# Moving output stores, one product order and one PSUM bank in a two-stage attention and maxout kernel

## The chip, the cores and the metric

One core of a Trainium2 chip. The metric is device time in microseconds (us), the median of several runs. A profiled execution gives the times of single instructions.

## The reference

Two layers follow each other. The first is a gated linear recurrence over 768 steps, for 4 batches of 8 heads with 48 features; the second is a feed-forward layer with a maximum over three products.

```python
f = 1.0 / (1.0 + np.exp(-f_logit))
for t in range(S):
    state = f[:, :, t, :, None] * state + np.einsum('bhd,bhe->bhde', k[:, :, t], v[:, :, t])
    y[:, :, t] = np.einsum('bhd,bhde->bhe', q[:, :, t], state)
x = y.transpose(0, 2, 1, 3).reshape(B * S, H * D)          # 3072 x 384
h = np.maximum(np.maximum(x @ w1, x @ w2), x @ w3)          # 3072 x 768
out = h @ w_out                                             # 3072 x 384
```

## The kernel before

**Units and groups.** The recurrence is worked off in 24 units (`u`). A unit holds 64 steps of two batches, so 128 tokens. Four units make a group (`g`, 0 to 5) of 512 tokens, and a group goes through the feed-forward layer as a whole. In the main loop one unit of the recurrence is computed while the feed-forward work of the group before it is fed in between.

**How the order is set.** The order on every engine is the order in which the Python program emits the instructions; nothing is rearranged later. The feed-forward work of a group is a generator (`ffn_first` for group 0, `ffn` for the others) that yields after each piece of TensorE work with that piece's cost. `fill(ns)` draws pieces from the first pending generator until the given time is spent. So the statement after a `yield` is emitted when the next piece is drawn. Engines run their own queue in order and wait for each other by semaphores. All loads and stores but a few are issued by SP, whose queue is in order as well.

**A unit.** `load` and `load_v` fetch f, k, q and v; from unit 6 on f, k and q come for two units at a time, in eight DMAs for each of the three. `sigmoids` (ACT), `scan` (DVE, L329), `after` (kt by a DVE transpose L296, then kh on POOL L340), `before` (prod by a DVE scan L347, qt by L296, qh on POOL L351), `keys_by_blocks` (ks, DVE L382, in four parts), `pairs` (PE L396, masked to `at` by DVE L399), `values` (PE L415, then a one-element ACT copy `seen`, L422), `sums` (PE L433) and `finish` (PE L504, then ACT copies into xT, L511). `pack` moves a part of xT between partitions by DMA (L524). "k(10)" below is the load of k for units 10 and 11, "pairs(10)" the pairs of unit 10.

**Group 0.** `ffn_first` computes products of xT with w2 and w3 (`product`, L542), and it turns each 128-column piece of w1 by three TensorE transposes and an ACT copy (`turn`, L779 and L780). `linear` folds w1 into w_out (L787). `outputs` computes the four output tiles of the group (L568), ACT copies each into the buffer `o_four` (the tile `o`, L572), and `store` issues two DMAs for each (L560). In the text, product (5,1) is the one of the last block with w2, (5,2) the one with w3.

**Groups 1 to 5.** `inputs_by_pairs` computes the maxout in three blocks (n = 0, 1, 2) of seven products each (L883), which saves multiplications by sums and differences of the operands: `start`, `plain`, `fifth`, `sixth`, `seventh`, `third`, `fourth`. ACT copies partial results (L891, L897, L906, L911, L918), POOL adds (L901, L919), DVE forms the maxima (L926, L933, L934), POOL then makes the sums that the output needs (`sums_of_hm`, L608). `outputs_by_pairs` computes the output in the same manner (L636) in PSUM banks a, b and c. ACT reads bank a into `partial` (L641), DVE or POOL add the parts into `o_four` (L644, L703). Only when they are computed are the four tiles of a group put on the list `late`, and `store_late` issues their eight DMAs in the next group.

**Banks.** A product's bank comes from the pool `ps_f` (name p, two banks) or `ps_tr` (name tr, two banks), each in rotation. A bank is written again only when its last reader is done:

```python
def bank(in_tr=False):
    if in_tr:
        return ps_tr.tile([128, TOK], FP32, name="tr")
    return ps_f.tile([128, TOK], FP32, name="p")
```

Of the kernel before, what the change touches and what calls it, by code (L numbers as in the profile page):

```python
# [9 lines left out]
FP32 = mybir.dt.float32  # L10
# [45 lines left out]
def kernel(  # L56
# [15 lines left out]
    NU = B // 2 * (S // C)  # L72
# [4 lines left out]
    NJ = DFF // 128  # L77
    GRP = 4
    TOK = GRP * UT
# [10 lines left out]
    def fast():  # L90
        ctx = ExitStack()
        with ctx:
# [4 lines left out]
            ps_f = ctx.enter_context(tc.tile_pool(name="ps_f", bufs=2, space=bass.MemoryType.PSUM))  # L97
# [417 lines left out]
            def by_halves(xT):  # L515

                return xT[:, 0:NK].rearrange("p k t -> p (k t)").rearrange("p (two k t) -> p two k t", two=2, k=NK)
# [14 lines left out]
# [4 lines that stand above are left out]
# [17 lines left out]
            def new_top(w):  # L553
                return work.tile([128, TOK], FP32, name="top")[:, 0:w]

            def store(u, o):
                c, bp = divmod(u, 2)
                for a in range(2):
                    t0 = (2 * bp + a) * S + c * C
                    nc.sync.dma_start(out=out[t0:t0 + C, :], in_=o[a * C:(a + 1) * C, :])  # L560

            def outputs(hm, xT, i):
                p = bank()
                t = slice(i % 2 * UT, (i % 2 + 1) * UT)
                terms = [(hm[:, j, i * UT:(i + 1) * UT], w_out[:, j, :]) for j in range(NJ)]
                terms += [(by_halves(xT)[:, i // 2, k, t], w_nat[:, k, :]) for k in range(NK)]
                for n, (lhsT, rhs) in enumerate(terms):
                    nc.tensor.matmul(p[:, 0:DM], lhsT=lhsT, rhs=rhs, start=(n == 0), stop=(n == NJ + NK - 1))  # L568
                    if n % NK == NK - 1:
                        if n == NJ + NK - 1:  # L570
                            o = o_four[:, i]
                            nc.scalar.copy(o, p[:, 0:DM])  # L572
                            store(i, o)
                        yield NK * DM * COLUMN


# [17 lines left out]
            def mix_x(n):  # L594

                of = lambda k, c: w_lin[:, k, c * HD:(c + 1) * HD]
                dst, x, y = ((x_mix[2], of(1, 1), of(0, 1)), (x_mix[0], of(0, 1), of(0, 0)),
                             (x_mix[1], of(1, 1), x_mix[0]), (x_mix[3], of(1, 0), x_mix[1]),
                             (w_mix[4][:, 2], of(2, 0), of(2, 1)))[n]
                nc.gpsimd.tensor_tensor(dst, x, y, op=ALU.subtract)  # L600
# [9 lines left out]
            def sums_of_hm(hm, jj):  # L610
                sums_of_pair(hm[:, 2 * jj], hm[:, 2 * jj + 1], *(t[:, jj] for t in s_mix))
# [7 lines left out]
            def outputs_by_pairs(g, hm, xT):  # L619
# [9 lines left out]
                lin, lin_mix = [[w_lin[:, 2, half(n)]] for n in range(2)], [w_mix[4][:, 2]]  # L629
                partial = [w_nat[:, n, :] for n in range(NK)]  # L630
                last = g == NU // GRP - 1
                begun = set()

                def into(b, p, lhs, rhs, part=slice(None)):
# [11 lines left out]
                def second():  # L646
                    for p in range(2):
                        into(a, p, s2, T(1))
                        if p:
                            read(a, 1)  # L650
                        yield COST
# [25 lines left out]
                    store_part(g, 0, 0)  # L677
                yield 2 * PART_COST
                d = b if last else c
                if last:  # L680
                    yield from second()
                into(c, 0, s1, T(0))
                yield COST
# [6 lines left out]
                else:  # L690
                    nc.scalar.copy(tops[:, 2], c[:, 0:DM])
                yield COST
                if not last:
                    yield from second()
                into(a, 0, A(0, 1), T(2))
                yield COST
# [49 lines left out]
            late = []  # L746

            def store_late():
                while late:
                    store(*late.pop(0))  # L750
# [22 lines left out]

            def turn(j):

                p = ps_f.tile([128, TOK], FP32, name="p")
                piece = w_in[0][:, :, j * 128:(j + 1) * 128]
                for a in range(NK):
                    nc.tensor.transpose(p[:, a * 128:(a + 1) * 128], piece[:, a, :], ident)  # L779
                nc.scalar.copy(piece, p[:, 0:DM].rearrange("q (a c) -> q a c", a=NK))  # L780
                yield DM * COLUMN
# [89 lines left out]
            def inputs_by_pairs(g, hm, xT):  # L871
                X = lambda k, h: halves(xT, k, h)
                t1, t2, t3, t4, t5 = sums_of_x(g)
                s1, s2, s4 = w_sum
                s3 = w_two[1][:, 0]
                COST = 2 * HALF * COLUMN
                out = lambda n, h: hm[:, 2 * n:2 * n + 2, h * HALF:(h + 1) * HALF]
                first, u3 = rests[:, 0:2, 0:HALF], tops[:, 2:4, 0:HALF]
                A, B, U5 = {}, {}, {}

                def into(b, n, w, x, begin=False):
                    for j in range(2):
                        nc.tensor.matmul(b[:, j * HALF:(j + 1) * HALF], lhsT=w[:, (2 * n + j) * 128:(2 * n + j + 1) * 128],  # L883
                                         rhs=x, start=begin and j == 0, stop=True, skip_group_check=True)

                def plain(n):
                    B[n] = bank(True)
                    into(B[n], n, w_two[0][:, 1], X(1, 0), True)
                    yield COST
                    into(B[n], n, w_two[0][:, 2], X(2, 0))  # L890
                    nc.scalar.copy(out(n, 0), two(B[n]))  # L891
                    yield COST

                def start(n):
                    A[n] = bank()
                    into(A[n], n, w_two[0][:, 0], X(0, 0), True)
                    nc.scalar.copy(first, two(A[n]))  # L897
                    yield COST

                def join(n):  # L900
                    nc.gpsimd.tensor_tensor(out(n, 0), out(n, 0), first, op=ALU.add)  # L901

                def fifth(n):
                    into(B[n], n, s1, t1, True)
                    U5[n] = two(new_top(TOK))
                    nc.scalar.copy(U5[n], two(B[n]))  # L906
                    yield COST

                def sixth(n):
                    into(A[n], n, s2, t2)  # L910
                    nc.scalar.copy(out(n, 1), two(A[n]))  # L911
                    yield COST

                def seventh(n):
                    into(A[n], n, s3, t3)
                    yield COST
                    into(A[n], n, w_two[1][:, 2], X(2, 1))
                    nc.scalar.copy(u3, two(A[n]))  # L918
                    nc.gpsimd.tensor_tensor(u3, u3, U5[n], op=ALU.add)  # L919
                    yield COST  # L920

                def third(n):
                    into(B[n], n, s4, X(1, 1))
                    yield COST
                    into(B[n], n, w_two[0][:, 2], X(2, 1))
                    nc.vector.tensor_tensor(out(n, 1), two(B[n]), out(n, 1), op=ALU.add)  # L926
                    yield COST

                def fourth(n):
                    into(A[n], n, w_two[1][:, 1], t4)  # L930
                    yield COST
                    into(A[n], n, w_two[1][:, 2], t5)
                    nc.vector.scalar_tensor_tensor(out(n, 0), out(n, 0), 0.0, two(A[n]), op0=ALU.max, op1=ALU.max)  # L933
                    nc.vector.scalar_tensor_tensor(out(n, 1), out(n, 1), 0.0, u3, op0=ALU.max, op1=ALU.max)  # L934
                    sums_of_hm(hm, n)
                    if g == 1:
                        for i in ((0, 1), (2, 3, 4), ())[n]:
                            mix_x(i)
                    yield COST

                yield from start(0)
                yield from plain(0)
                join(0)
                store_late()
                yield from plain(1)
                yield from sixth(0)
                yield from fifth(0)
                for n in range(1, NJ // 2):
                    if n > 1:
                        yield from plain(n)  # L950
                    yield from seventh(n - 1)
                    yield from start(n)
                    join(n)
                    yield from third(n - 1)
                    yield from fifth(n)
                    yield from sixth(n)
                    yield from fourth(n - 1)
                yield from seventh(NJ // 2 - 1)
                yield from third(NJ // 2 - 1)
                yield from fourth(NJ // 2 - 1)  # L960
# [452 lines left out]
```

## Time and profile before

| what | value |
|---|---|
| median of three runs | 413.81 us (413.4 to 414.51) |
| the profiled execution | 413.13 us, span 411.4 us |
| granted TensorE clock | 0.998 |
| PE busy (matmuls) | 392.9 us, 96% of the span |
| DVE busy | 294.6 us, 72% |
| POOL busy | 245.7 us, 60% |
| ACT busy | 180.8 us, 44% |
| moved by DMA | 47.21 MB, mean 115 GB/s |

The span is the time from the first to the last instruction; the execution takes 1.73 us more. PE is the TensorE matmul, PEld its weight load, DVE is VectorE, ACT ScalarE, POOL GpSimd, and SPq the queue of SyncE, which here only issues DMAs. L560 is line 560 of the kernel. A PE row's end is modelled, and the rows of neighbouring matmuls overlap.

### The profile page before, as it was taken

To read this page: it belongs to the slowest core of one execution; us is meant where nothing else is said; L and a number is where in the kernel's file an instruction comes from. 1 tells how busy PE (TensorE), PEld (TensorE's weight loads), DVE (VectorE), ACT (ScalarE), POOL (GpSimd) and SP (SyncE) were. 2 spreads that over 40 slices of the span, in tenths; PEclk is the share of its full clock that TensorE was granted. 3 is DMA by queue.
4 is the path that set the end of the run, shared out by engine and by line. 5 is a ranking of instruction groups with operands and counts; after the bars stand their busy time and mean duration, and the time that the engine had idled before them with its cause. 6 is when DMAs were issued, how large, how long until landed. Compare 5 with 4: busy or idle time off the path is not lost.

```text
span 411.4 us, 11515 instructions
## 1 busy us (share of the span) xinstructions
PE 392.9 (96%) x4598; PEld 331.9 (81%) x4598; DVE 294.6 (72%) x569; ACT 180.8 (44%) x430; POOL 245.7 (60%) x270
## 2 busy tenths in 40 slices
PE   5988999999999989999999999999999999999995
PEld 4766765556678778998889998899988899988994
DVE  6997897996885899898898997998995450002500
ACT  2478786412224422425542345522354424586210
POOL 2189694843878777577495296667377850435700
PEclk9999999999999999999999999999999999999999
DMA  8999986776456775266655277734473003542012
GB/s 172 240 269 261 271 222 92 149 149 94 87 112 89 124 119 108 60 91 108 108 137 110 47 115 88 158 74 86 64 152 101 2 17 102 126 135 67 0 21 62
DMA packets 181562, 47.21 MB, mean 115 GB/s; under 512 B 160448, under 2 KB 179200, under 8 KB 181504
## 3 DMA queue, kind: packets, MB, share of 16 engines
q1 hardware_dynamic: 178032, 45.62, 54.1%
q10 hardware_dynamic: 3472, 0.81, 0.9%
q8 instruction: 37, 0.61, 0.6%
q14 instruction: 21, 0.17, 0.1%
HBM read 37.75 MB, written 4.72 MB: 103 GB/s over the span
## 4 chain that ended last, share of the span: by engine, by line
PE 85%; DVE 6%; POOL 3%; issue 2%; DMA 1%; ACT 1%; SPq 0%; DVEq 0%; POOLq 0%
PE p L883 17%; PE tr L883 15%; PE p L636 14%; PE tr L636 10%; PE p L542 7%; PE p L568 6%; PE p L787 3%; PE y L415 3%; PE a L396 3%; PE a L433 2%; PE y L504 2%; DVE ks L382 2%; PE tr L291 1%; POOL w_in L258 1%; DMA f_ld<-in_f_logit_dram 1%
## 5 line engine op out<-in xcount | busy, mean ns | idle before, releaser
L382 DVE STREAM_TRANSPOSE ks<-kh 32x128 f32<-32x128 f32 x256 | 77.3, 302 | 10.3 <-POOL kh L340 6.3
L883 PE MATMUL tr<-xT,placed 128*128 128x256 f32 x300 | 71.1, 382 | 0.0
L883 PEld LDWEIGHTS tr<-xT,placed 128*128 128x128 f32 x300 | 56.3, 190 | 8.0
L883 PE MATMUL p<-xT,placed 128*128 128x256 f32 x180 | 44.6, 379 | 0.0
L339 POOL COPY ends<-r 128x8 f32<-128x8 f32 x24 | 6.9, 288 | 56.9 <-DVE r L329 56.9
L340 POOL TENSOR_TENSOR kh<-kt,r 128x512 f32<-128x512 f32 x18 | 33.4, 1855 | 10.6 <-DVE kt L296 10.6
L883 PEld LDWEIGHTS p<-xT,placed 128*128 128x128 f32 x180 | 34.1, 190 | 4.7
L329 DVE TENSOR_TENSOR_SCAN r<-gate,from_one 128x520 f32<-128x520 f32 x24 | 33.4, 1391 | 5.9 <-ACT gate L308 2.8
L542 PE MATMUL p<-xT,w_in 128*128 128x256 f32 (+1 forms) x108 | 34.0, 459 | 3.4 <-POOL w_in L756 1.9
L511 ACT COPY xT<-y 64x256 f32<-64x256 f32 (+1 forms) x60 | 22.1, 369 | 23.3 <-PE y L504 22.6
L347 DVE TENSOR_TENSOR_SCAN prod<-gate,from_inv 128x520 f32<-128x520 f32 x24 | 30.5, 1269 | 0.0
L883 PE MATMUL p<-w_in,placed 128*128 128x256 f32 x120 | 30.4, 382 | 0.0
L644 DVE TENSOR_TENSOR o<-tr,w_in 128x384 f32<-128x384 f32 (+1 forms) x11 | 5.7, 521 | 34.3 <-PE tr L636 29.8
L608 POOL TENSOR_TENSOR w_in<-hm 128x256 f32<-128x256 f32 x15 | 11.1, 738 | 32.1 <-DVE hm L934 29.4
L542 PEld LDWEIGHTS p<-xT,w_in 128*128 128x128 f32 x108 | 19.5, 190 | 12.6 <-issue 6.0
L926 DVE TENSOR_TENSOR hm<-tr,hm 128x512 f32<-128x512 f32 x15 | 10.2, 683 | 23.1 <-ACT raw L280 17.2
L258 POOL TENSOR_TENSOR w_in<-top_bits,rest_bits 128x384 uint32<-128x384 uint32 x18 | 21.7, 1217 | 7.2 <-DVE top_bits L252 4.3
L883 PEld LDWEIGHTS p<-w_in,placed 128*128 128x128 f32 x120 | 22.4, 190 | 4.4 <-issue 1.3
L636 PE MATMUL p<-w_in,hm 128*128 128x192 f32 x120 | 25.3, 334 | 0.6 <-ACT w_in L641 0.6
L641 ACT COPY w_in<-p 128x384 f32<-128x384 f32 x15 | 7.2, 479 | 42.1 <-PE p L636 42.1
L280 ACT ACTIVATE raw<-top_bits 128x384 f32<-128x384 f32 x48 | 25.3, 526 | 0.4
L636 PE MATMUL tr<-w_out,w_in 128*128 128x192 f32 x120 | 24.4, 326 | 0.0
(156 smaller groups left out, 912.3 us busy)
## 6 DMA issues: line engine op xcount, KB each, us to landing
raw<-in_moe_w_dram SPq DMA_DIRECT2D x24, 384.0 KB, 4.2
v_ld<-in_v_dram SPq DMA_DIRECT2D x48, 96.0 KB, 3.3
placed<-in_moe_w_dram SPq DMA_DIRECT2D x12, 384.0 KB, 6.8
out_dram<-o SPq DMA_DIRECT2D x46, 96.0 KB, 2.2
placed<-in_moe_w_out_dram SPq DMA_DIRECT2D x6, 384.0 KB, 5.5
f_ld<-in_f_logit_dram SPq DMA_DIRECT2D x36, 64.0 KB, 2.7
k_ld<-in_k_dram SPq DMA_DIRECT2D x36, 64.0 KB, 2.6
q_ld<-in_q_dram SPq DMA_DIRECT2D x36, 64.0 KB, 2.6
```

What stands on the lines that cost most here:

```text
L258: nc.gpsimd.tensor_tensor(dst, by(top), by(rest), op=ALU.add)
L280: nc.scalar.activation(over, size, AF.Relu, scale=(-1 / HI_MIN, 1.0)[step - 1], bias=(1.0, -HI_END * (1 - 2.0 ** -24))[step - 1], accum_ou ...
L329: nc.vector.tensor_tensor_scan(r[:, 0:LEN][:, ::-1], flat(gate)[:, ::-1], flat(from_one)[:, ::-1], 1.0, op0=ALU.mult, op1=ALU.max)
L340: (nc.vector if u < BY_ROWS else nc.gpsimd).tensor_tensor(kh.rearrange("p h a t -> p a h t"), kt, by_batch(r[:, 1:LEN + 1].rearrange("p (x ...
L347: nc.vector.tensor_tensor_scan(flat(prod), flat(gate_tiles[u % 2]), flat(from_inv[u % 2]), 1.0, op0=ALU.mult, op1=ALU.max)
L382: nc.vector.transpose(ks[n * 32:(n + 1) * 32, :, par, e0:e0 + 32], kh[p0:p0 + 32, :, a, t0:t0 + 32])
L396: nc.tensor.matmul(p[t, par, hp * C:(hp + 1) * C], lhsT=kh[r, hp, a, :], rhs=qh[r, a, hp, :], start=True, stop=True)
L511: nc.scalar.copy(xT[o, :, t0 + a * C:t0 + (a + 1) * C], y[i, a, 0:HP * C].rearrange("p (h t) -> p h t", h=HP))
L542: nc.tensor.matmul(p if w < TOK else p.rearrange("p (two t) -> p two t", two=2), lhsT=w_in[i][:, kt, j * 128:(j + 1) * 128], rhs=x[:, t.st ...
L568: nc.tensor.matmul(p[:, 0:DM], lhsT=lhsT, rhs=rhs, start=(n == 0), stop=(n == NJ + NK - 1))
L636: nc.tensor.matmul(b[:, p * HD:(p + 1) * HD], lhsT=x, rhs=w, start=id(b) not in begun, stop=True, skip_group_check=True)
L883: nc.tensor.matmul(b[:, j * HALF:(j + 1) * HALF], lhsT=w[:, (2 * n + j) * 128:(2 * n + j + 1) * 128], rhs=x, start=begin and j == 0, stop= ...
```

## The change

There are three edits.

The four output tiles of group 0 are no longer stored by `outputs` when they are copied. They are put on `late`. In group 1 `store_late` is not called behind `join(0)`; it is called at the end of each turn of the loop over the blocks, so the eight DMAs are issued where the piece after the first block's last product (`fourth(0)`) is drawn. In groups 2 to 5 the call stays behind `join(0)`.

In `outputs_by_pairs` the two products with s2 (`second`) come ahead of the two with s1 in groups 4 and 5. Before, they did so in group 5 alone.

The last turn of a w1 piece (j = 5) takes its bank from the pool `ps_tr` instead of `ps_f`.

```diff
@@ outputs
                             nc.scalar.copy(o, p[:, 0:DM])
-                            store(i, o)
+                            late.append((i, o))
@@ outputs_by_pairs
                 last = g == NU // GRP - 1
+                tight = g >= NU // GRP - 2
...
                 d = b if last else c
-                if last:
+                if tight:
                     yield from second()
                 into(c, 0, s1, T(0))
...
-                if not last:
+                if not tight:
                     yield from second()
                 into(a, 0, A(0, 1), T(2))
@@ turn
-                p = ps_f.tile([128, TOK], FP32, name="p")
+                p = bank(j == NJ - 1)
@@ inputs_by_pairs
                 join(0)
-                store_late()
+                if g > 1:
+                    store_late()
                 yield from plain(1)
...
                     yield from sixth(n)
                     yield from fourth(n - 1)
+                    store_late()
                 yield from seventh(NJ // 2 - 1)
```

## The prediction

> **What bounds the kernel now.** First the page's busy row, then busy time by stage, with the stages cut where the maxout groups 1 to 4 begin on PE:
>
> ```profile
> PE 392.9 (96%) x4598; PEld 331.9 (81%) x4598; DVE 294.6 (72%) x569; ACT 180.8 (44%) x430; POOL 245.7 (60%) x270
> ...
> 118.47:180.89 62.42, 59.35 (x773) 53.32 (x773) 52.70 (x108) 23.86 (x57) 44.02 (x47) 1.00 0.59 100
> 180.89:239.38 58.49, 58.49 (x773) 53.20 (x773) 52.65 (x113) 24.42 (x60) 38.22 (x42) 1.00 0.57 99
> 297.89:356.19 58.30, 57.73 (x677) 51.85 (x677) 25.95 (x45) 26.01 (x67) 35.26 (x39) 1.00 0.32 79
> ```
>
> Columns: window, length, then busy us (and instructions) of PE, PEld, DVE, ACT, POOL, granted clock, DMA share, GB/s. PE is the bound, so a saving is worth the PE idle time that it removes. Group 1 runs the same 773 matmuls as group 2 and takes 62.42 - 58.49 = **3.93 us longer**, 3.07 of it visible as idle PE (62.42 - 59.35). Group 2 has no gap, group 4 has 0.57.
>
> Then PE's timeline, for the gaps (start, length, line; in brackets the idle time before and its releaser):
>
> ```profile
> 74.19 2.84 PE L542 MATMUL p<-xT,w_in 128*128 128x512 f32 x6 [0.35 <-ACT hm L807]
> ...
> 136.48 0.69 PE L396 MATMUL a<-qh,kh 48*64 48x64 f32 x32 [0.83 <-POOL qh L351]
> ...
> 153.87 0.66 PE L504 MATMUL y<-qh,state 48*48 48x64 f32 x32 [1.54 <-ACT seen L422]
> ...
> 161.71 1.19 PE L636 MATMUL p<-w_out,hm 128*128 128x192 f32 x4 [0.70 <-DVE hm L933]
> ...
> 345.98 0.92 PE L636 MATMUL p<-w_in,hm 128*128 128x192 f32 x4 [0.57 <-ACT w_in L641]
> ```
>
> Between 59.5 and 404 us PE has hardly another gap. For what is behind the first of group 1's, SP's timeline and DVE's:
>
> ```profile
> 113.74 1.33 SPq L164 DMA_DIRECT2D v_ld<-in_v_dram  x2
> 115.17 3.26 SPq L560 DMA_DIRECT2D out_dram<-o  x4
> 118.52 1.35 SPq L524 DMA_DIRECT2D xT<-xT  x2
> 119.96 1.40 SPq L164 DMA_DIRECT2D v_ld<-in_v_dram  x2
> 121.45 1.23 SPq L560 DMA_DIRECT2D out_dram<-o  x2
> 122.81 5.24 SPq L183 DMA_DIRECT2D k_ld<-in_k_dram  x8
> 128.14 4.15 SPq L183 DMA_DIRECT2D q_ld<-in_q_dram  x8
> 132.39 1.12 SPq L560 DMA_DIRECT2D out_dram<-o  x2
> ...
> 130.23 0.71 DVE L296 STREAM_TRANSPOSE kt<-k_ld 128x512 f32<-128x512 f32 x1 [2.55 <-DMA q_ld<-in_q_dram]
> 134.46 0.71 DVE L296 STREAM_TRANSPOSE qt<-q_ld 128x512 f32<-128x512 f32 x1 [2.39 <-DMA out_dram<-o]
> ```
>
> SP issues without a pause here, well behind the data: the pack at 118.52 copies an xT that ACT finished at 109.80. So k and q of units 10 and 11 are issued late. DVE idles 2.55 us for k and 2.39 for q (the profile names the last DMA event, a store, but qt reads q_ld, whose last issue ended at 132.29), POOL then makes qh, and pairs(10) waits for qh. The 4.9 us that DVE lost come back twice: DVE is nearly full from 135 to 162, and its late L934 holds ACT's copy L918 (5.94 us), behind which the small `seen` copy stands that releases L504; its late L933 gives the third gap. With the slow restart behind each, the excess of 3.93 divides so: the unit work from L415 to L504 takes 2.01 in group 2 (197.11 to 199.12 in the chain of waits), here 3.04 (134.51 to 137.55) and 3.76 (150.70 to 154.46), which is 1.03 and 1.75; 1.15 is left for the third.
>
> **What the Trainium skill says.** "Perfetto Trace Analysis", section "DMA Instruction — HWDGE (DVE, Sync)": a DMA's row starts when its semaphores are satisfied and ends when the sequencer is free for the next; moving the data lies outside. The trace agrees: q's rows take about 0.5 us, its data lands a median 2.5 us after issue. Section "What "DMA-bound" means" of that page lists an issuing sequencer that is solid with DMA rows as a bound of its own; SP from 108.8 to 148 is that, while the DMA share is 0.48 to 0.93. "PSUM — Partial Sum Buffer", section "Engine vs sequencer instructions": ACT, DVE and POOL queues are strict FIFO, and matmuls complete in program order. L918 ahead of `seen` is such a case.
>
> **The change, part by part.**
>
> *The last turn's bank.* Today product (5,1), the turn and product (5,2) take three of the two p banks in a row, so (5,2) at 74.19 waits for the copy L807 of (5,1), 73.55 to 74.14. With the turn in a tr bank, (5,2) takes the bank that L809 left at 71.73. The two tr banks were last read by DVE L351 (to 61.6) and ACT L369 (to 67.9), and are next asked for at 119, so the turn doesn't wait at 73.35. Linear(0) then needs the bank of (5,1), free at 74.14, and w1's last piece at its sixth matmul, about 78.1, copied by 75.96. Gain **0.35**; no new wait.
>
> *The stores.* Eight DMAs leave three places on SP. What follows starts earlier by 118.52 - 115.17 = 3.35, then 122.81 - 121.45 = 1.36, then 133.56 - 132.39 = 1.17, together 5.88. k(10) and q(10) are issued 4.71 earlier; their rooms were last read for unit 7 (DVE, before 104), so nothing else holds them. k's data is there at 130.23 - 4.71 = 125.5, q's at 134.46 - 4.71 = 129.75. DVE: its reciprocal ends at 127.68, kt to 128.4, prod 1.20 to 129.5, qt 129.75 to 130.4. POOL: the pack is 3.35 earlier, so L867's wait of 1.24 goes and all behind moves up by it: ends to 128.8, kh 2.02 to 130.8, qh 1.18 to 132.0. PE reaches pairs(10) at 135.65 - 0.35 = 135.3: 3.3 of slack, the 0.83 goes.
>
> What is late next is DVE's L933, which needs fourth(0) on PE, done at 134.2. L933 0.65, L934 1.3, a quarter of ks 1.26: at(10) starts at 137.4 instead of 141.53, 4.1 earlier. From at(10) to the release of L504 by `seen` the trace has 153.87 - 141.53 = 12.34: 149.8. PE is there at 152.33 - 0.83 - 0.35 = 151.15; the 1.54 goes with 1.4 of slack. The third: L933 of the last block ended at 161.65, now 157.5; PE comes at 161.01 - 2.72 = 158.3 by the visible gaps, at 157.9 with the slow restarts behind them. Slack 0.4 to 0.8, the thinnest; I leave a remainder of 0 to 0.5 here. So group 1 gains between 3.07 (gaps only) and 3.93 (as fast as group 2); I take **3.5**.
>
> The eight DMAs come back on SP where plain(2) of group 1 begins, behind v(12): v(12) ended at 152.4, now 146.5. Eight such stores in one burst take 5.07 at 303.84, so to 151.6. Behind them stand one check load (152.41 before), the pack of units 8 to 10, which waits for ACT until 155.38 before and about 152.3 after, and f(14) at 157.83. SP idled 2.35 ahead of that pack, so the burst fits where the gap and the 5.88 are. Who waits for the stores: DVE L644 of group 1, which overwrites `o`, due near 159; landing by 153.8 (2.2 after issue). Cost 0, covered by 5 us; at SP's old times the stores would land at 159.6 and cover nothing.
>
> *s2 first in group 4.* Today bank a carries s2 and then the next product back to back, so PE waits 0.57 for ACT's reading L641 (345.45 to 345.93). With s1's two products (2.6 us) between, that wait is hidden. The new place of s2 follows the reading of a at 338.81 to 339.29; between stand finish(23) (0.6) and b's rest (0.65), so s2 is due at 340.05: 0.7 of slack. Its POOL sums were ready at 335.97, its DVE ones at 336.3. In group 5, already in this order but without a finish between, the first s2 block is 0.25 longer, which bounds the cost; I take 0. L691's copy comes 2.6 later and is needed by bank c's next product, 3.3 after it. Gain **0.6** (0.57, and 0.11 for a slower restart). Group 5 doesn't change.
>
> **Sum:** 0.35 + 3.5 + 0.6 = 4.45; from 3.1 + 0.35 + 0.3 = 3.75 to 3.93 + 0.45 + 0.68 = 5.06. The profiled execution took 413.13 (span 411.4 and 1.73 around it); the sum makes it 408.7. The median is 0.68 above, so **409.4** there, full case 408.7 to 410.1.
>
> **Rivals.** *Half:* DVE, busy 26.8 of the 28 us from 136 to 164, doesn't catch up, and of the second and third gap half stays, or all: 1.03 for the first, 1.45 or 0 for the rest, 0.95 for the other two parts, 410.4 or 411.8. For it: the slack of 0.4. Against: group 2 does the same DVE work (52.65) in 58.49 without a gap. *Hidden anyway:* k and q are held by something else than the stores, or the stores aren't issued later, so only 0.95 is gained: 412.9. For it: the 16 DMA engines are at 0.93 near 136 to 140. Against: 0.48 and 0.53 at 120 to 128, where the loads move to. *Slower:* `o` becomes the wait. If SP doesn't run ahead, DVE's L644 waits in line for the last store to land, and behind it the sums of xT, kt(12) and qt(12), so pairs(12) on PE. Each us past 159 is a us; it has to use up 4.5 first, so it decides from a landing after 163.5, and a landing at 165 gives 415.3. Against: it needs SP over 10 us later than worked out.
>
> **How the numbers follow.** Full 0.66 (409.4), half 0.15 (411.1), hidden 0.10 (412.9), slower 0.09. Range 408.6 to 411.9: the full and half cases with their bounds. About 0.3% (1.24 us) is what a measurement of this kernel can tell from no change; full and half lie beyond it.
>
> **What would show it.** On SP no store between v(9) and k(10), k(10) issued near 118, and one run of eight stores near 146 to 152; no idle DVE before kt and qt of unit 10; no gap at pairs(10), at L504 behind `seen`, at product (5,2), and between s2 and the next product of group 4; group 1 in 58.5 to 59.3. A gap left at L636 with releaser L933 is the remainder. It is wrong if kt(10) still waits for its load, or if DVE L644 waits for an out_dram DMA.

## The result and the profile after

The changed kernel takes 409.05 us in the median (408.47 to 409.97, four runs) against 413.94 before (413.40 to 414.51): a ratio of 0.988, with a 95% interval of 0.986 to 0.991. The profiled execution took 408.62 with a span of 406.9, so 4.5 less than the one shown before. In it the time falls into four stretches: up to the last turn on PE 73.28 us (73.35 before), from there to group 2's first product 103.95 (107.54 before), groups 2 and 3 unchanged at 117.00, group 4 57.46 (58.30 before), and 55.21 from there to the end, unchanged. The gain is 3.59 ahead of group 2 and 0.84 in group 4. Of the 3.59, 0.50 lies between the last turn and group 1's first product (45.12 before, 44.62 now) and 3.09 in group 1 itself (62.42 before, 59.33 now). (In the changed file the lines behind L631 are higher by one to three: L883 is now L884, L933 L934, L636 L637, L644 L645.)

The stages of the kernel after, in the same columns as before: the window's length, then busy us of PE, PEld, DVE, ACT and POOL.

```profile
117.90:177.23 59.33, 58.91 (x773) 53.14 (x773) 51.66 (x108) 23.87 (x57) 44.23 (x47) 1.00 0.63 109
177.23:235.72 58.49, 58.49 (x774) 53.20 (x773) 52.62 (x113) 24.41 (x60) 38.24 (x42) 1.00 0.57 100
294.23:351.80 57.57, 57.57 (x678) 51.95 (x678) 25.96 (x45) 26.02 (x67) 35.26 (x39) 1.00 0.33 81
```

The last window runs 0.11 beyond group 4, which ends at 351.69. Group 1 is still 0.84 longer than group 2; group 4 has no idle PE any more. On PE's timeline of the kernel after, from the last turn on:

```profile
73.28 0.49 PE L780 MATMUL tr<-ident,w_in 128*128 128x128 f32 x3
73.61 2.74 PE L542 MATMUL p<-xT,w_in 128*128 128x512 f32 x6
...
134.91 0.66 PE L396 MATMUL a<-qh,kh 48*64 48x64 f32 x32
...
150.54 0.63 PE L504 MATMUL y<-qh,state 48*48 48x64 f32 x32
...
157.15 0.49 PE L637 MATMUL tr<-w_in,xT 128*128 128x192 f32 x2
158.05 1.20 PE L637 MATMUL p<-w_out,hm 128*128 128x192 f32 x4 [0.41 <-DVE hm L934]
...
336.39 0.81 PE L637 MATMUL p<-w_in,w_in 128*128 128x192 f32 x4
```

Product (5,2) follows the turn at once, pairs(10) and L504 of unit 10 wait for nothing, and s2's first product of group 4 (at 336.39) has no wait ahead of it either. One gap is left, the third, with 0.41 and the releaser L934. SP's queue and DVE in the kernel after, for what stands behind it:

```profile
113.24 1.33 SPq L164 DMA_DIRECT2D v_ld<-in_v_dram  x2
114.67 1.30 SPq L524 DMA_DIRECT2D xT<-xT  x2
116.06 2.12 SPq L164 DMA_DIRECT2D v_ld<-in_v_dram  x2
118.28 5.48 SPq L183 DMA_DIRECT2D k_ld<-in_k_dram  x8
123.88 4.26 SPq L183 DMA_DIRECT2D q_ld<-in_q_dram  x8
...
146.23 5.66 SPq L560 DMA_DIRECT2D out_dram<-o  x8
```

DVE's timeline of the same kernel:

```profile
126.14 0.71 DVE L296 STREAM_TRANSPOSE kt<-k_ld 128x512 f32<-128x512 f32 x1 [0.17 <-DMA q_ld<-in_q_dram]
130.78 0.71 DVE L296 STREAM_TRANSPOSE qt<-q_ld 128x512 f32<-128x512 f32 x1 [2.74 <-DMA q_ld<-in_q_dram]
...
157.32 0.67 DVE L934 SCALAR_TENSOR_TENSOR hm<-hm,p 128x512 f32<-128x512 f32 x1
```

k's loads are issued 4.53 earlier (118.28 against 122.81), q is used 3.68 earlier (130.78 against 134.46), and the last block's maximum comes 3.65 earlier (157.32 against 160.97). The moved stores stand in one run at 146.23.

One sign that the prediction named did not come: DVE was to have no idle time ahead of kt and qt, and it still waits 2.74 for q. That is the clue to what follows, since it means that q still sets DVE's pace. Ahead of kt the wait fell from 2.55 to 0.17 (to 0.79, for k, in the second profile below). Group 1's 59.33 lies at the upper end of the 58.5 to 59.3 that were forecast.

### The profile page after: what moved, and what is told of

Same layout as the page of the kernel before. It is cut to its first block, busy times and chain, and to the rows that moved or that the text cites. A ratio compares the mean times of both kernels' runs of the same rounds, so it can differ in the third digit from the quotient of the medians.

```text
span 406.9 us, 11516 instructions
## 1 busy us (share of the span) xinstructions
PE 391.8 (96%) x4598; PEld 331.6 (81%) x4598; DVE 293.8 (72%) x569; ACT 180.7 (44%) x430; POOL 246.1 (60%) x270
## 4 chain that ended last, share of the span: by engine, by line
PE 82%; DVE 8%; issue 2%; SPq 2%; POOL 2%; ACT 1%; DMA 1%; DVEq 0%
PE p L884 16%; PE p L637 15%; PE tr L884 13%; PE tr L637 11%; PE p L542 7%; PE p L568 6%; PE p L788 3%; PE y L415 3%; PE a L396 2%; PE a L433 2%; SPq L183 2%; DVE ks L382 2%; PE y L504 2%; DVE r L329 2%; PE tr L367 1%
## 5 line engine op out<-in xcount | busy, mean ns | idle before, releaser
L884 PE MATMUL tr<-xT,placed 128*128 128x256 f32 x300 | 71.1, 382 | 0.0
L884 PEld LDWEIGHTS tr<-xT,placed 128*128 128x128 f32 x300 | 56.3, 190 | 8.0
L884 PE MATMUL p<-xT,placed 128*128 128x256 f32 x180 | 44.6, 379 | 0.0
L884 PEld LDWEIGHTS p<-xT,placed 128*128 128x128 f32 x180 | 34.1, 190 | 4.7
L329 DVE TENSOR_TENSOR_SCAN r<-gate,from_one 128x520 f32<-128x520 f32 x24 | 32.3, 1345 | 5.9 <-ACT gate L308 2.9
L884 PE MATMUL p<-w_in,placed 128*128 128x256 f32 x120 | 30.4, 382 | 0.0
L645 DVE TENSOR_TENSOR o<-tr,w_in 128x384 f32<-128x384 f32 (+1 forms) x11 | 5.7, 521 | 33.8 <-PE tr L637 29.4
L884 PEld LDWEIGHTS p<-w_in,placed 128*128 128x128 f32 x120 | 22.4, 190 | 4.4 <-issue 1.5
L637 PE MATMUL p<-w_in,hm 128*128 128x192 f32 x120 | 25.2, 333 | 0.0
L637 PE MATMUL tr<-w_out,w_in 128*128 128x192 f32 x120 | 24.4, 326 | 0.0
```

What stands on the lines that cost most here:

```text
L329: nc.vector.tensor_tensor_scan(r[:, 0:LEN][:, ::-1], flat(gate)[:, ::-1], flat(from_one)[:, ::-1], 1.0, op0=ALU.mult, op1=ALU.max)
L637: nc.tensor.matmul(b[:, p * HD:(p + 1) * HD], lhsT=x, rhs=w, start=id(b) not in begun, stop=True, skip_group_check=True)
```

## The experiments

Three theories were set against each other. **A**: SP's queue sets when q of unit 10 arrives, and from there a chain on DVE sets when group 1 ends; what PE saves ahead of that is lost. **B**: the three parts add up gap by gap, as in the prediction's sum. **C**: the stores delay the loads by their bytes on the DMA engines, not by their place in SP's queue.

The kernel before was measured again beside them. Its median was 414.30 in the runs of the first four (turn, s2, stores, all three), 414.00 in those of the next four and 413.86 in those of the last three; each ratio is against its own. The ratios and their intervals are worked out over all runs, so they can differ a little from the quotient of two medians.

One number carries most of what follows, the time from the start of qt(10) on DVE to group 2's first product on PE. SP's queue stands up to 3 us earlier or later at the same place from one execution to the next (its first move of w_in's pieces, L458, begins between 100.68 and 103.75 in these profiles). The number from qt(10) on doesn't move with it. All from one profiled execution each; "second profile" is that of all three parts run again below:

| kernel | last turn to qt(10) | qt(10) to group 2 | last turn to group 2 |
|---|---|---|---|
| before | 61.11 | 46.43 | 107.54 |
| changed kernel, first profile | 57.50 | 46.45 | 103.95 |
| changed kernel, second profile | 59.42 | 46.43 | 105.85 |
| turn alone | 62.50 | 46.42 | 108.92 |
| s2 alone | 61.29 | 46.86 | 108.15 |
| stores alone | 58.31 | 46.45 | 104.76 |
| half of the stores | 61.98 | 46.88 | 108.86 |
| stores of group 0 left out | 57.27 | 46.44 | 103.71 |
| stores one place later | 58.03 | 46.45 | 104.48 |
| narrow stores | 62.51 | 46.42 | 108.93 |
| v behind q | 54.75 | 48.24 | 102.99 |
| v behind q, turn as before | 56.00 | 47.51 | 103.51 |

In eight of the twelve rows it is 46.42 to 46.45. The four others are explained below: two by PE's clock, two because q no longer sets the pace. With all stores at their old place (before, turn alone, s2 alone, narrow stores) q comes 61.11 to 62.51 after the last turn, with all of them moved or left out and v where it was (both profiles of the changed kernel, stores alone, stores left out, one place later) 57.27 to 59.42. The means are 61.85 and 58.11, so q's lead is 3.75 on average.

**The turn alone.**

```diff
-                p = ps_f.tile([128, TOK], FP32, name="p")
+                p = bank(j == NJ - 1)
```

> Only the last turn takes a tr bank; stores and s2 as before. Theory A (the arrival of q for unit 10, set by SP's queue, sets through DVE's chain when group 1's outputs begin, so what PE saves ahead of it is lost): the gap of 0.35 at product (5,2) goes, but the gap at pairs(10) grows from 0.83 to 1.0 to 1.2, and the time stays within 0.2 us of before. Theory B (the three parts add up, as the prediction's sum has it): 0.35 less, group 1's gaps unchanged.

Measured: 414.13, ratio 1.000 (0.998 to 1.002). On its PE timeline the gap at product (5,2) is gone, a new one has come, and the one at pairs(10) has grown from 0.83:

```profile
133.06 1.13 PE L883 MATMUL p<-xT,placed 128*128 128x256 f32 x4 [0.42 <-ACT rest_bits L897]
...
138.33 0.69 PE L396 MATMUL a<-qh,kh 48*64 48x64 f32 x32 [1.33 <-POOL qh L351]
```

The arrival of q was itself 1.39 later in this execution, counted from the last turn, and pairs(10) came 1.39 later with it (64.52 after the turn, 63.13 before). What PE had saved went into waiting, here and in the new gap of 0.42, where L883 waits for ACT's L897. From qt(10) to group 2 it takes 46.42, as before. So the profile speaks for A: alone, the turn's bank is worth nothing. The times can't show it, since their interval is 0.8 to either side.

**s2 alone.**

```diff
-                if last:
+                if tight:
                     yield from second()
```

> Only the order in group 4 is changed. Both theories: the gap of 0.57 ahead of the product after s2 goes, group 4 takes 57.6 instead of 58.3, group 1 keeps its three gaps; about 0.6 to 0.7 us less than before. If the wait only moves: a gap of the same size ahead of the first s2 product, and no gain.

Measured: 412.90, ratio 0.997 (0.995 to 0.998). The gap is gone, no new one stands ahead of s2, and group 4 takes 57.46 (357.13 - 299.67) instead of 58.30. It is worth 0.84, not the 0.57 that the gap shows; by the ratio the times fell by 1.4, between 0.7 and 2.0. In the row of the table 46.86 is 0.43 too long, and so it is for half of the stores: in both, PE's granted clock fell for a moment behind the long gap at L504, and its matmuls took longer. The stage table of this kernel over five us there, with the mean granted clock as the third number from the right:

```profile
155.00:160.00 5.00, 4.78 (x45) 4.06 (x46) 4.84 (x14) 2.43 (x8) 4.84 (x9) 0.66 0.47 126
```

The mean hides two levels: from 156.3 to 159.7 the granted clock was 0.50, outside of that 1.00.

**The stores alone, and all three again.**

```diff
-                            store(i, o)
+                            late.append((i, o))
...
-                store_late()
+                if g > 1:
+                    store_late()
...
                     yield from fourth(n - 1)
+                    store_late()
```

> Only the stores are moved. Theory A: qt of unit 10 comes 3.7 us earlier and group 1's L933 of the last block with it, so the gain is 3.5 to 3.7 without the turn, and the gap at the first output product with hm's last pair is under 0.15, since PE comes 0.35 later than with all three parts; product (5,2) keeps its 0.35. Theory B: 3.1 less, the gap at the output product stays at 0.4.

> The three parts together, beside the single ones. Theory A: the time of the stores alone less 0.6 to 0.7 for s2, and nothing for the turn: 4.3 less than before. Theory B: the sum of the three, of which the turn is 0.35.

Measured: the stores alone 410.58, ratio 0.994 (0.990 to 0.998); all three 410.43 in the same runs, ratio 0.991 (0.988 to 0.994). DVE and PE of the stores alone:

```profile
131.64 0.71 DVE L296 STREAM_TRANSPOSE qt<-q_ld 128x512 f32<-128x512 f32 x1 [2.24 <-DMA q_ld<-in_q_dram]
...
158.18 0.67 DVE L933 SCALAR_TENSOR_TENSOR hm<-hm,p 128x512 f32<-128x512 f32 x1
...
158.91 1.20 PE L636 MATMUL p<-w_out,hm 128*128 128x192 f32 x4 [0.70 <-DVE hm L933]
```

By the ratio the stores alone gain 2.5, between 0.8 and 4.2. That holds A's 3.5 to 3.7 and B's 3.1 alike, so the profiles have to tell them apart. My expectation of under 0.15 for the last gap was wrong here: q came 0.86 later than in the first profile of all three, the gap is 0.70, and DVE's L933 comes 26.54 after qt, as in the kernel after (26.54) and before (26.51). Where q was in time with the turn as before, in the kernel without these stores below (57.27), no gap stands there. In the second profile of all three q came later still (qt at 133.53), a wait of 1.39 was back at L504, and the span was 409.7. Against the profile of before the same kernel thus gains 3.59 in one execution and 1.69 in another ahead of group 2, and q came 1.92 later in the second (59.42 against 57.50 after the turn), which is the whole of the difference. That is A; in B's sum the gaps would have sizes of their own.

**The same stores on ACT's queue.**

```diff
-                            store(i, o)
+                            store(i, o, nc.scalar)
```

> The kernel before, with the eight stores of group 0 at their old place in the program, but issued by ACT instead of SP. Theory A (SP's queue: the seconds that SP spends on issuing delay q): k and q of unit 10 are issued 4.7 us earlier than before, near 118 and 123, qt starts 3.5 to 4 earlier, L933 of the last block 26.5 after qt as ever, and the time is that of the stores moved alone, 3.1 to 3.7 less than before, less what ACT's eight issues of 0.6 cost it (0 to 1). Theory C (the stores' bytes compete with the loads on the DMA engines): the same bytes move at nearly the same time, qt stays within 1 us of before, no gain.

Measured: 433.27, ratio 1.046 (1.043 to 1.049). Neither theory was tested. SP got a new wait, by its own list of waits:

```profile
SPq L465 <- DMA out_dram<-o: 16.2, 2, 11.7
```

Two of SP's moves of weight pieces (L465) waited 16.2 us for ACT's stores, and k and q of units 8 and 9 behind them made PE wait 15.35 at pairs(8). The moves and the stores have no data in common, so something else in the program ties DMAs of the two queues together. The trace shows the wait and not what that is.

**Half of the stores.**

```diff
-                            store(i, o)
+                            late.append((i, o)) if i > 1 else store(i, o)
```

> The kernel before, with only the stores of the last two tiles of group 0 moved; the first two stay. Theory A: of the two stores' four issues two stand ahead of k and q, so q comes 1.36 us earlier, L933 of the last block with it (26.5 after qt), and the time is 1.3 to 1.4 less. Theory B (gap by gap, each with its own slack): the gap at pairs(10) goes and gives about 1.0, the two later gaps stay as they are.

Measured: 413.62, ratio 0.998 (0.996 to 1.000), that is 0.8 less, between 0.1 and 1.5. Its profile fell on an execution with SP late; counted on SP from the first move of w_in's pieces (L458) to k's first issue, it gains 21.75 - 20.63 = 1.12 of the 1.36. The gap at pairs(10) was 1.11. That doesn't refute B, for in this execution q came 0.87 later than in the profile of before, counted from the last turn, and not earlier. The interval holds A's 1.3 to 1.4 and B's 1.0, so this experiment doesn't decide between them.

**The stores left out, and one place later.** The first leaves group 0's rows unwritten. The second is the changed kernel with the burst behind the last block of group 1's maxout.

```diff
-                            store(i, o)
+                            pass
```

> The kernel before, with the stores of group 0 left out altogether (its output rows are not written). If the moved stores cost nothing at their new place, this has the time of the stores moved alone, within 0.5: 3.2 to 3.7 less than before. If the burst of eight at the new place holds the pack or later loads, this one is faster than that by what it costs.

```diff
                     yield from fourth(n - 1)
-                    store_late()
...
                 yield from fourth(NJ // 2 - 1)
+                store_late()
```

> All three parts, but the eight stores stand one place later, behind the last block of group 1's maxout. On SP they then follow v of unit 13, near 161 to 166, and land near 168, while DVE's first overwriting of the buffer o is due near 166 to 168. The rival slower case of the prediction: DVE waits 1 to 2.5 us for an out_dram DMA at that instruction. If DVE has slack there, PE gets no gap and the time is that of all three parts; if not, it is 1 to 2 longer.

Measured: left out 410.16, ratio 0.992 (0.988 to 0.995), against 410.58 for the stores alone; 46.44 from qt(10) to group 2. So the burst costs nothing at its new place that can be seen. One place later 409.45, ratio 0.988 (0.985 to 0.992). SP and DVE of that kernel:

```profile
161.60 5.23 SPq L560 DMA_DIRECT2D out_dram<-o  x8
...
168.13 0.56 DVE L645 TENSOR_TENSOR o<-tr,w_in 128x384 f32<-128x384 f32 x1
```

Issued 15 us later than in the kernel after, the stores are still done in time: L645 waits for no DMA and stands 35.06 after qt(10), in both kernels. The rival slower case is more than 15 us away, though perhaps hardly more. The last of the eight is issued from 166.2 to 166.83, and these stores land 2.2 us after issue in the median, so by this estimate the last one lands between 168.4 and 169.0. L645, which overwrites two of the four tiles, begins at 168.13. A still later burst wasn't tried.

**Narrow stores.** The kernel before, but each of group 0's eight stores writes 16 of its 384 columns.

```diff
-                            store(i, o)
+                            store(i, o, 16)
```

> The kernel before, but group 0's eight stores, at their old place, write only the first 16 of the 384 columns: the same number of DMAs and rows on SP, a 24th of the bytes (the rest of group 0's rows is not written). Theory A (SP's issue time): qt of unit 10 stays within 1 us of before, the gaps stay, the time is within 0.7 of before. Theory C (bytes on the DMA engines): qt 3 us or more earlier, and 3 us less.

Measured: 413.21, ratio 0.999 (0.997 to 1.002). With a 24th of the bytes SP takes as long, and q isn't earlier:

```profile
117.10 3.31 SPq L560 DMA_DIRECT2D out_dram<-o  x4
...
135.97 0.71 DVE L296 STREAM_TRANSPOSE qt<-q_ld 128x512 f32<-128x512 f32 x1 [2.73 <-DMA out_dram<-o]
```

3.31 for four issues against 3.26 for the full ones. SP stood later in this execution; counted from L458 to the end of q's issues it took 31.45, and 31.23 before. C falls: it is the time of issuing, not the bytes. The number of rows in each store was the same, so a cost of each row isn't told apart from one of each DMA.

**v behind q.** The changed kernel, with v of units 9 and 10 issued behind q of unit 10, once with all three parts and once with the turn as before.

```diff
-                    if u + 2 < NU:
+                    if u + 2 < NU and u not in (BY_ROWS + 1, BY_ROWS + 2):
                         load_v(u + 2)
...
                         load(u + 2, one, "q")
+                    if u == BY_ROWS + 2:
+                        load_v(u + 1)
+                        load_v(u + 2)
```

> All three parts, and v of units 9 and 10 issued behind q of unit 10 instead of ahead of k. Theory A: q arrives 2 to 3.5 us earlier still, so DVE's wait ahead of qt (2.7) goes; from there PE's fourth(0) is what DVE's L933 of the first block waits for, so the chain gains only 0.5 to 0.8 more: the last gap at the first output product with hm's last pair (0.41 to 0.70) goes, and from the last turn to group 2's first product it takes 103.0 to 103.4 (all three parts: 103.95 in the first profile, 105.85 in the second). Theory B, for which q has slack since the move: no change.

> As the kernel with v behind q, but the last turn in a p bank as before. With q early, PE is the limit of group 1. Theory A: then, and only then, the turn's bank is worth its gap: 0.35 longer than with the turn's tr bank from the last turn to group 2's first product (103.4 to 103.8), while it was worth nothing alone. If q still sets the end, both take the same.

Measured: 408.32, ratio 0.987 (0.984 to 0.989), and 408.55, ratio 0.987 (0.985 to 0.990). DVE of the first:

```profile
131.24 0.68 DVE L296 STREAM_TRANSPOSE qt<-q_ld 128x512 f32<-128x512 f32 x1
137.32 0.69 DVE L934 SCALAR_TENSOR_TENSOR hm<-hm,p 128x512 f32<-128x512 f32 x1 [1.48 <-PE p L884]
```

qt waits for nothing now, and the releaser of the first block's maximum is PE: DVE waits 1.48 for fourth(0). PE has no gap in all of group 1, which takes 58.38 (121.10 to 179.48), as long as group 2. Here the turn's bank counts: 102.99 with it, 103.51 without, so 0.52, where it was worth nothing while q was late. These are one profile each; the times of the two, 408.32 and 408.55, don't tell them apart. By the times alone the version with v behind q isn't clear of the changed kernel; it is the fastest by its median, and by the table it leaves group 1 nothing more to lose.

## Why the prediction was right, and where a step was off

The time fell inside the range, 0.35 below the forecast, and the main mechanism was the one that was forecast: SP issues k and q earlier, so DVE and PE lose less. Not forecast was that q would still set the end of group 1. Step by step:

- **SP's queue.** Forecast: k near 118.1, v(12) done by 146.5, the burst to 151.6. Measured: 118.28, 146.18, 146.23 to 151.89. q was forecast in DVE's hands at 129.75 and came at 130.78: k's and q's sixteen issues stretched to 9.86 (9.48 before), and from the end of the issuing to qt it took 2.64 instead of 2.17. So q's lead was 3.68 of the 4.71 worked out.
- **Group 1.** Forecast 3.5, between 3.07 and 3.93. Measured from the last turn 3.59. But the step was wrong in its form. The prediction carried q's lead along DVE to each wait and set it against PE's arrival there; at the last one it had DVE done 0.4 to 0.8 ahead of PE, so it took PE for the limit and summed PE's gaps. In the run DVE's L934 of the last block ended at 157.99 (157.5 worked out), and PE was there at 157.64 (157.9 to 158.3 worked out). So DVE was still the later one, and the table shows the consequence: 46.4 from qt(10) to group 2 as long as DVE waits for q, so the gain is q's lead, whatever it is in an execution. It was the place that the prediction called thinnest, with a remainder of 0 to 0.5; 0.41 came, and 0.70 in other executions.
- **The turn.** The term of 0.35 was mis-sized. By the constant stretch it is worth 0 in this kernel, as q sets the end; where PE does, it is worth 0.52.
- **s2.** Forecast 0.6, measured 0.84. No new wait came, as forecast. The term was too small because I took the idle time of 0.57 and 0.11 for the restart. Counted from start to start, the last product ahead of the gap and the one behind it are further apart: A's four products of L636 that follow s2 begin at 345.98, where 345.25 would have been due by the 2.60 that each earlier sixteen took. That is 0.73, the idle 0.57 and the 0.16 by which a PE row otherwise begins ahead of the modelled end of the row before it (342.65 against 342.81). With the 0.11 it is 0.84.
- **The overwriting of o.** "Due near 159" was a plain error: in the trace before, L644 of group 1 runs at 169.50, and it needs only the bank of group 1's first output part. The cover was more than twice the 5 us that I counted: the burst lands near 154 (its end and the median 2.2, an estimate), and the overwriting stands at 165.84. With the burst one place later, about all of it is used up by the estimate above, and still L645 doesn't wait.
- **Rivals.** Half: not taken, though the second profile of all three comes near it, by q's arrival and not because DVE couldn't catch up. Hidden anyway: excluded, since k's issue moved by 4.53 and q's use by 3.68 once the stores were gone from ahead of them; the narrow stores exclude that bytes held them. Slower: it didn't come, not even with the later burst.

So the sum of 4.45 agrees with the profile's 4.5 in part by compensation: 0.35 too much for the turn, 0.24 too little for s2, and 3.59 where 3.5 stood; 0.07 of the 4.5 lies ahead of the last turn. How near the time came was also luck: the same kernel run again gave 410.43, 3.7 less than before by the ratio, between 2.6 and 4.9.

What stays open is why SP's queue stands differently from one execution to the next. At the first move of w_in's pieces it is at 100.68 in the first profile of the changed kernel and at 103.10 in the second. Nothing here tells where those 2 us arise.

## What to carry to other kernels

Look for a stretch of constant length between an event on one engine and the end of the stage on another: it tells which resource sets the pace, and it holds where the times scatter more than the effect. A gap that is removed ahead of such an event is worth nothing until the event itself comes earlier, so move first what stands in the queue ahead of the late load: stores whose data nobody waits for, and loads that are needed later. And count a gap from start to start of the work around it, not by its idle time.

## What the runs showed of the hardware

- A store of 64 rows costs SP the same with 64 bytes to a row as with 1536: four took 3.31 us (narrow stores) and 3.26 us (before).
- Idle times of 0.35 and 0.57 us on PE cost 0.52 and 0.84. In the profile a PE row begins about 0.16 ahead of the modelled end of the row before it where nothing waits, so the idle time shown is short by that.
- PE's granted clock can fall to 0.50 for 3.4 us behind a short gap: from 156.3 to 159.7 behind the gap of 1.54 at L504 (s2 alone), and likewise behind 1.56 (half of the stores), with 0.4 us lost up to group 2. In the profiles of before, the turn alone and the narrow stores the same gap, of 1.53 to 1.54, had no such moment, so the gap alone doesn't bring it about; what else does isn't known.
